# Eight more weight loads in 8 KB reads, two modes per product, and a reordered tail in a windowed-attention and spectral-mix kernel

## The chip, the cores and the metric

One Trainium2 chip, one of its eight cores. The time is device microseconds of one execution, and the median over several executions is given. Lower is better. The profile is of one execution. TensorE is called PE, VectorE DVE, ScalarE ACT, GpSimd POOL and SyncE SP; PEld is PE's loading of the stationary operand. DMAs issued by POOL run in queue q0, those of SP and ACT in q1.

## The reference

```python
# q, k, v: 8 batches x 8 heads x 576 positions x 64, fp32
scores = q @ k.T / 8, kept where 0 <= row - column < 64, else -1e9
x = softmax(scores) @ v              # heads side by side: 8 x 576 x 512
X = rfft(x, axis=1)[:, 0:64]         # 64 modes, complex
Yr = Xr @ w_r - Xi @ w_i             # a 512 x 512 matrix of its own for each mode
Yi = Xr @ w_i + Xi @ w_r
y = irfft(Y, n=576)                  # other modes zero
u = x + y
out = u + relu(u @ w_ch)             # w_ch 512 x 512, fp32
```

The 64 modes have two fp32 matrices each, 128 MiB in all; q, k and v are 27 MiB, the output is 9 MiB.

## The kernel before

Weights are read once. POOL's DMAs cast them from fp32 to bf16 on the way, so 1 MB written means 2 MB read. The modes come in 16 groups of four. Groups 0 to 9 are worked in two halves of the input channels, `hb` 0 (channels 0 to 255) and `hb` 1 (256 to 511); groups 10 to 15 as pairs of whole modes. `wlist` holds the loads in order: first halves of groups 0 to 9 (w_r, w_i each), second halves of groups 0 to 9, then the pairs, the last four pairs of groups (`LAST`, `LAST + 1`) at the end. `load_weights(n)` issues them in this order as far as buffers (`ringA`, `ringB`, lent regions) are free; `due(it)` sets how many are wanted in each step of the attention.

The stage under `manual_schedule` runs attention in 40 units (loop over `it`): transposes of q, k and v (L298), scores (L337, L345), row maxima on DVE (L349), maxima subtracted by a product (L357), exp on ACT (L359), transposes of the weights (L365, L368), product with v (L385, L391, L397), and the forward transform of a batch's half (`do_dft`, L408 and L410, copied by ACT in L413 and L414 to `XQ`). From unit 22 on, `early_step` also does the first half of one group: `mode_half` (L223), 8 products a part (w_r, w_i), each of one mode and 128 channels with 32 columns, on four column groups of PE; the sum goes to `Yacc` (L542). Program order fixes the order on each engine; the engines wait for each other by semaphores, and POOL issues in its program's order.

Then come the second halves. Those of groups 0 and 1 are like the first. Those of groups 2 to 9 (`WIDE = 2`) are loaded by L195: one DMA of 512 KB for two modes, in which a partition reads four rows of a matrix, 8 KB; even partitions hold the one mode and odd ones the other. For that, `wide_modes` spreads the modes' spectra to every second partition, with zeros between (`sprE`, L722 to L741), in `XE`; `mode_wide` (L231) then does one product per mode, in which the other mode's partitions meet zeros: 16 products a part. Loads of L203 (halves of groups 0 and 1, and all first halves) read two rows, 4 KB, per partition and mode; loads of the pairs (L184) read 8 KB.

During the second stage the other work is put between: x times w_ch (L678, L653, L685, L942), inverse tables, and for each group the rows of the spectrum turned (`finish_group`, L755). With the pairs, `mode_pair` (L254) and `finish_pair` do the same; `jobs` holds the products with w_ch of the spectrum's rows (L836, L825, L826), the early sums of x and y (L900, L907) and so on.

The tail begins with the last pair's part: `finish_pair` copies its sum (L770), `turn` transposes it (L785), `put_first` (L790) and `take` (L796) place it; it is multiplied with w_ch (L1205), and `cast_halves` (L702, L703) copies that to `ZL`, the late rows of Z. YL (L1201) holds the late rows of Y. Then tiles of 128 output rows are finished in pairs: `tail_xw` (L976) puts x w_ch in a PSUM bank, `late_u` (L986) and `late_z` (L993) add the late rows for u and for u w_ch, `take_u` (L1007, DVE) and `take_z` (L1011 ACT, L1012 POOL, L1014 DVE) finish them, and SP sends them (L1003). Later tiles go through `full_u` and `full_z` with all rows at once (L1029 to L1063), and `last` does the last pair.

At the very start, eight products of zeros, 128 x 512 each (L432), keep PE busy while the first loads come.

Of the kernel before, what the change touches and what calls it, by code (L numbers as in the profile page):

```python
# [9 lines left out]
FP32 = mybir.dt.float32  # L10
FP32R = mybir.dt.float32r
BF16 = mybir.dt.bfloat16
# [4 lines left out]

NRA = 3
NRB = 5
WARM = 8  # L20
NEG = -1.0e30
MAGIC = 12582912.0
PSAFE = 3.14159
# [3 lines left out]
def kernel(  # L27
# [10 lines left out]
    nc = tc.nc  # L38
# [64 lines left out]
    XA = XA[:, 0:(3 * NW + 2) * B * NMF].rearrange("p (s b m) -> p s b m", b=B, m=NMF)  # L103
    steps += [(grp, hb) for grp in (*range(EARLY, LAST), *range(LAST + 2, NGRP), LAST, LAST + 1) for hb in range(2)]
    WIDE = 2
    NE = 2 * (EARLY - WIDE)
    SHARES = 25, 11, 80, 12
    assert sum(SHARES) == 128
    XE = XE[:, 0:2 * (3 * NW + 2) * B * NE].rearrange("p (h s b m) -> p h s b m", h=2, b=B, m=NE)
    ONES = 3, 0  # L110
    wlist = []
    for at, (grp, hb) in enumerate(steps):
# [37 lines left out]
    def load_weights(n):  # L150
        nonlocal nload
        while nload < len(wlist):
            at, parts, hb, ri = wlist[nload]
            if 2 * n <= sum(len(ps) for ps in parts):
                return
            if nload in lent:
                w = lent[nload]
            else:
                open_to = "a" if at >= 2 * EARLY else "aby" if at < EARLY + 2 else "ab"
                h = min(open_to, key=lambda h: held[h][0] if len(held[h]) == room[h] else -1)  # L160
                if len(held[h]) == room[h]:
                    if held[h][0] not in spent:
                        return
                    held[h].pop(0)
                held[h].append(nload)
                if h == "y":
                    w = lentY
                else:
                    w = {"a": ringA, "b": ringB}[h].tile([128, 4, NJ, DM], BF16, name="wi" if ri else "wr", tag="wt")
            src = moe_w_i if ri else moe_w_r  # L170
            if at >= 2 * EARLY:
                w = w.rearrange("p (m h) j e -> p m (h j) e", m=2)
                p = parts[0][0]
# [13 lines left out]
                wtiles.update(((p + m, ri), w[:, m]) for m in range(2))  # L187
                nload += 1
                n -= 2
                continue  # L190
            if at >= EARLY + WIDE:
                w = w.rearrange("p (q h) j e -> p q (h j e)", q=2)
                for i in range(2):
                    p = parts[0][2 * i]
                    nc.gpsimd.dma_start(  # L195
                        out=w[:, i], in_=src[p:p + 2, HALF:DM, :].rearrange("h (p j) e -> p h (j e)", j=NW))
                    wtiles[p, hb, ri] = w[:, i].rearrange("p (j e) -> p j e", j=NW)
                nload += 1
                n -= 4
                continue  # L200
            to = 0
            for ps in parts:
                nc.gpsimd.dma_start(  # L203
                    out=w[:, to:to + len(ps)],
                    in_=src[ps[0]:ps[-1] + 1, HALF * hb:HALF * hb + HALF, :].rearrange("g (p j) e -> p g j e", j=NJ))
# [25 lines left out]
    def mode_wide(psm, at, ri):  # L231
        grp, hb = steps[at]
        for j in range(NW):
            for g in range(4):
                nc.tensor.matmul(out=psm[32 * g:32 * g + 32, :],  # L235
                                 lhsT=XE[:, g % 2].rearrange("k s b m -> k (s b) m")[:, (3 * j + 1 - ri) * B:(3 * j + 5 - ri) * B,
                                                                                    2 * (grp - WIDE) + g // 2],
                                 rhs=wtiles[4 * grp + g - g % 2, hb, ri][:, j], start=(ri == 0 and j == 0),
                                 stop=(ri == 1 and j == NW - 1), tile_position=(0, 32 * g))
        for i in range(2):  # L240
            wtiles.pop((4 * grp + 2 * i, hb, ri))
        spend(at, ri)

    def mode_pair(psm, at, ri):
        grp, h = steps[at]
# [16 lines left out]
    with tc.manual_schedule():  # L262
# [2 lines left out]
        trigF = maskp.tile([128, NTF, 2 * NM], BF16, name="trigF")  # L265
        mask_t = maskp.tile([128, 3, 4, 128], BF16, name="mask_t")
        rawp = pool("rawp", bufs=2)
        qtp = pool("qtp", bufs=3)
        vtp = pool("vtp")
        vdp = pool("vdp")  # L270
# [158 lines left out]
        nc.vector.memset(idle, 0.0)  # L429
        warm = ps_m.tile([128, DM], FP32, name="warm", tag="misc")  # L430
        for _ in range(WARM):
            nc.tensor.matmul(out=warm, lhsT=idle[:, 0:128], rhs=idle, start=True, stop=True)  # L432

        casts = list(load_by_sp(0, "k", Vflat[1])) + list(load_by_sp(0, "q", Vflat[2]))
        nc.gpsimd.iota(Kf, pattern=[[1, 64]], base=0, channel_multiplier=0,
# [166 lines left out]
        sprE = XL.rearrange("p s b m -> p (s b m)")[:, 0:512].rearrange("p (r h k) -> p r h k", r=2, h=2)  # L602
# [97 lines left out]

        def cast_halves(out, in_):
            nc.vector.tensor_copy(out=out[:, 0:HALF], in_=in_[0][:, 0:HALF])  # L702
            nc.scalar.copy(out=out[:, HALF:DM], in_=in_[1][:, 0:HALF])  # L703

        def whole_modes():
            pts = [[bank("zt"[r == 0]) for j in range(NJ)] for r in range(2)]
# [12 lines left out]
                    nc.vector.tensor_scalar(out=XA[:, i], in0=px[:, 1], scalar1=-1.0, scalar2=None, op0=ALU.mult)  # L719

        def wide_modes():
            nc.vector.memset(sprE, 0.0)  # L722
            for r in range(2):
                for h in range(2):
                    nc.vector.tensor_copy(out=sprE[:, r, h, h::2], in_=ident_bf[:, r::2])
            pts = [[bank("zt"[r == 0]) for j in range(NJ)] for r in range(2)]
            for r in range(2):
                for j in range(NJ):
                    for h in range(2):
                        nc.tensor.matmul(  # L730
                            out=pts[r][j][:, 2 * B * NE * h:2 * B * NE * (h + 1)], lhsT=sprE[:, r, h],
                            rhs=XQ[1][:, 3 * j + 1:3 * j + 3, :, 4 * WIDE:4 * EARLY].rearrange(
                                "p t b (m h) -> p (t b) m h", h=2)[:, :, :, h],
                            start=(h == 0), stop=True, skip_group_check=True)
            nc.vector.memset(XE[:, :, 3 * NW:], 0.0)
            for r in range(2):
                for j in range(NJ):
                    i = 3 * (NJ * r + j)
                    px = pts[r][j].rearrange("p (h t b m) -> p h t b m", h=2, t=2, b=B)
                    nc.scalar.copy(out=XE[:, :, i + 1:i + 3], in_=px)  # L740
                    nc.vector.tensor_scalar(out=XE[:, :, i], in0=px[:, :, 1], scalar1=-1.0, scalar2=None, op0=ALU.mult)  # L741
            lo = 4 * (LAST - EARLY)
            nc.vector.tensor_copy(out=XL, in_=XA[:, :, :, lo:lo + 8])

# [21 lines left out]
        def finish_pair(grp, h, psm):  # L766
            if h == 0:
                late["stg"] = stgpool.tile([128, DM], BF16, name="stg")
            stg = late["stg"][:, HALF * h:HALF * h + HALF]
            nc.vector.tensor_copy(out=stg, in_=psm[:, 0:HALF])  # L770
# [490 lines left out]
```

## Time and profile before

| | |
|---|---|
| median of 3 runs | 430.76 us (430.76 to 431.33) |
| the profiled execution | 430.37 us, its span 428.6 us |
| PE busy | 341.0 us, 80% |
| DVE, ACT, POOL busy | 247.1, 184.6, 113.2 us |
| q0 (POOL's DMAs) | 31424 packets, 81.80 MB written |
| read from HBM | 163.58 MB, 404 GB/s over the span |
| attention ends | about 191 us |
| last weights land | 393.7 us |

GB/s in slices and windows is what the DMA engines write; a casting load reads twice that. The busy share of DMA is a mean over 16 engines and can pass 1, since an engine has several packets under way. In the windows the columns are the stretch, its length, busy time (and instructions) of PE, PEld, DVE, ACT and POOL, the clock granted to PE, the DMA share and GB/s. In the waits a line gives who waited for whom, the sum in us, how often, and the longest. In the timeline a line gives start, duration, engine, line, operation, what is written and read, and in brackets the engine's idle time before and who ended it.

### The profile page before, as it was taken

Reading aid. Unit: us, or ns where it says so; the run is one execution under the profiler, and the core shown is the slowest. Engines: PE = TensorE matmul, PEld = TensorE weight load, DVE = VectorE, ACT = ScalarE, POOL = GpSimd, SP = SyncE. Lnnn points to the kernel's source line nnn. Section 1 sums busy time; section 2 is a strip of 40 time slices with the busy share of each in tenths; the row PEclk is TensorE's granted clock in tenths of the full one; section 3 lists DMA queues with packets and bytes.
Section 4 is the critical chain, followed back from the end, with each engine's and each line's share of the span. In section 5 each row is a group of like instructions: output and inputs, shape, how many; then the busy total and the mean of one; then the engine's idle time right before and its main releaser. Section 6 shows DMA issues by size and latency. Waiting matters only on the chain.

```text
span 428.6 us, 11742 instructions
## 1 busy us (share of the span) xinstructions
PE 341.0 (80%) x5098; PEld 224.9 (52%) x5142; DVE 247.1 (58%) x527; ACT 184.6 (43%) x334; POOL 113.2 (26%) x174
## 2 busy tenths in 40 slices
PE   6889989898999998987628577669675668878994
PEld 3656767676767676663204233346454445445552
DVE  8688777877677675784503212033322333886995
ACT  5655757575676566532401101025222214233663
POOL 8313223222122132112222222121111111120994
PEclk9999999999999999985657767689999986999998
DMA  8999999999999999999999999999999999996698
GB/s 206 211 211 212 211 212 210 212 211 212 211 211 212 213 213 210 213 213 214 213 255 220 213 213 214 207 211 214 214 215 214 214 214 214 213 210 119 241 364 299
DMA packets 37188, 93.30 MB, mean 218 GB/s; under 512 B 2992, under 2 KB 3248, under 8 KB 37136
## 3 DMA queue, kind: packets, MB, share of 16 engines
q0 software_dynamic: 31424, 81.80, 97.9%
q1 hardware_dynamic: 5568, 10.62, 6.8%
q8 instruction: 40, 0.66, 0.6%
q10 hardware_dynamic: 144, 0.13, 0.1%
q14 instruction: 12, 0.10, 0.1%
HBM read 163.58 MB, written 9.44 MB: 404 GB/s over the span
## 4 chain that ended last, share of the span: by engine, by line
DMA 43%; PE 39%; DVE 8%; issue 6%; ACT 3%; POOL 0%; DVEq 0%; SPq 0%; POOLq 0%; ACTq 0%
DMA wr<-in_moe_w_r_dram 23%; DMA wi<-in_moe_w_i_dram 16%; PE tr L298 6%; PE s L345 5%; DMA rawk<-in_k_dram 4%; PE s L357 4%; PE pt L365 4%; PE vb L310 3%; PE o L385 3%; PE s L337 2%; PE psm L223 2%; PE psz L685 2%; PE psm L254 2%; DVE xw L888 1%; PE px L408 1%
## 5 line engine op out<-in xcount | busy, mean ns | idle before, releaser
L685 PE MATMUL psz<-wch,tr 128*128 128x512 f32 x176 | 58.6, 462 | 10.8 <-DMA wch<-in_moe_w_ch_dram 10.0
L349 DVE TENSOR_REDUCE mx<-s 128x4 fp32r<-128x512 f32 x72 | 49.6, 688 | 25.5 <-PE s L345 25.2
L942 DVE CAST xw<-psz 128x512 fp32r<-128x512 f32 x36 | 24.9, 692 | 67.7 <-PE psz L685 67.7
L653 ACT CAST tr<-ptx 128x512 fp32r<-128x512 bf16 x36 | 21.2, 590 | 78.4 <-PE ptx L678 78.4
L359 ACT ACTIVATE p<-s 128x512 bf16<-128x512 f32 x72 | 39.7, 603 | 13.0 <-PE s L357 13.0
L685 PEld LDWEIGHTS psz<-wch,tr 128*128 128x128 f32 x176 | 34.4, 216 | 17.4 <-issue 10.2
L345 PE MATMUL s<-kT,qT 64*64 64x128 bf16 (+1 forms) x576 | 29.2, 221 | 6.7 <-issue 6.7
L302 ACT COPY kT<-tr 128x576 bf16<-128x576 bf16 x32 | 23.2, 724 | 21.4 <-PE tr L298 21.4
L368 DVE COPY pts<-pt 128x1024 bf16<-128x1024 bf16 (+1 forms) x40 | 25.2, 630 | 5.8 <-PE pt L365 4.3
L302 ACT COPY qT<-tr 128x576 bf16<-128x576 bf16 x32 | 23.3, 727 | 11.5 <-PE tr L298 11.5
L235 PEld LDWEIGHTS <-XQ 128*32 128x32 bf16 x256 | 11.4, 147 | 31.9 <-issue 25.5
L345 PEld LDWEIGHTS <-qT 64*64 64x64 bf16 x576 | 18.0, 107 | 17.7 <-issue 17.2
L357 PE MATMUL s<-mx,ident_r 128*128 128x512 f32 x72 | 26.2, 437 | 0.0
L302 ACT COPY vT<-tr 128x576 bf16<-128x576 bf16 x32 | 23.3, 728 | 4.7 <-PE tr L298 4.5
L285 POOL DMA_DIRECT2D rawk<-in_k_dram x15 | 8.1, 538 | 64.3 <-PE tr L298 56.3
L365 PE MATMUL pt<-ident_bf,p 128*128 128x128 bf16 x288 | 23.3, 220 | 1.8 <-issue 1.6
L747 DVE TENSOR_TENSOR stg<-psm,Yfour 128x512 bf16<-128x512 f32 x10 | 6.9, 689 | 30.6 <-PE psm L235 27.1
L254 PEld LDWEIGHTS <-XQ 128*32 128x32 bf16 x256 | 9.4, 149 | 28.4 <-issue 28.1
L235 PE MATMUL psm<-wi,XQ 128*32 128x512 bf16 x128 | 14.9, 507 | 10.5 <-DMA wi<-in_moe_w_i_dram 10.5
L184 POOL DMA_DIRECT2D wi<-in_moe_w_i_dram x14 | 9.5, 683 | 50.2 <-PE psm L254 29.1
L397 DVE TENSOR_TENSOR x_sb<-o,r 128x512 bf16<-128x512 f32 x32 | 22.1, 691 | 1.1
L235 PE MATMUL psm<-wr,XQ 128*32 128x512 bf16 x128 | 15.1, 540 | 7.4 <-DMA wr<-in_moe_w_r_dram 5.4
(277 smaller groups left out, 710.0 us busy)
## 6 DMA issues: line engine op xcount, KB each, us to landing
wi<-in_moe_w_i_dram POOLq DMA_DIRECT2D x21, 1024.0 KB, 14.3
wr<-in_moe_w_r_dram POOLq DMA_DIRECT2D x18, 1024.0 KB, 13.7
wi<-in_moe_w_i_dram POOLq DMA_DIRECT2D x17, 512.0 KB, 19.4
wr<-in_moe_w_r_dram POOLq DMA_DIRECT2D x16, 512.0 KB, 19.4
out_dram<-ut SPq DMA_DIRECT2D x29, 256.0 KB, 3.4
rawv<-in_v_dram POOLq DMA_DIRECT2D x16, 288.0 KB, 15.9
rawk<-in_k_dram POOLq DMA_DIRECT2D x15, 288.0 KB, 14.6
rawq<-in_q_dram POOLq DMA_DIRECT2D x15, 288.0 KB, 14.6
```

The lines of the kernel that those rows point to most:

```text
L235: nc.tensor.matmul(out=psm[32 * g:32 * g + 32, :], lhsT=XE[:, g % 2].rearrange("k s b m -> k (s b) m")[:, (3 * j + 1 - ri) * B:(3 * j + 5 ...
L298: nc.tensor.transpose(out=pt[ro, j, :], in_=raw[ro, TH * half + j, :], identity=ident_bf[ro, ro])
L302: nc.scalar.copy(out=to, in_=pt.rearrange("p j n -> p n j"))
L345: nc.tensor.matmul(out=s[ro, t, lo:128], lhsT=lq, rhs=kT[ro, 64 * n - 64 + lo:64 * n + 64], start=False, stop=True, skip_group_check=True)
L349: nc.vector.tensor_reduce(out=mx, in_=s, axis=AX.X, op=ALU.max, negate=True)
L357: nc.tensor.matmul(out=s, lhsT=ident_r, rhs=mx.unsqueeze(2).to_broadcast([128, 4, 128]), start=False, stop=True, skip_group_check=True)
L359: nc.scalar.activation(out=p[:, 4 * c2:4 * c2 + 4, :], in_=s, func=ACT_F.Exp, scale=EX_SCALE)
L365: nc.tensor.transpose(out=pt[:, t, :], in_=st[u]["p"][:, t, :], identity=ident_bf)
L368: nc.vector.tensor_copy(out=ps[:, 0:nt, :], in_=pt[:, 0:nt, :])
L397: nc.vector.tensor_tensor(out=xo.rearrange("p c (h d) -> p c h d", d=64), in0=ov[:, :, :, 0:64], in1=rb, op=ALU.mult)
L685: nc.tensor.matmul(out=pz, lhsT=tr[:, c, :], rhs=wch[:, c, :], start=(c == 0), stop=(c == NDCH - 1))
L942: nc.vector.tensor_copy(out=XW[i], in_=multiply(tr))
```

## The change

- First halves of groups 6 to 9 (`FIRST_WIDE = 6`) are loaded as the second halves of 2 to 9 are: two DMAs of 512 KB in place of one of 1 MB, 8 KB read per partition and mode. `early_step` uses `mode_wide` for them.
- Before step 6's product, in the step of group 5, `spread_modes` spreads the first halves' spectra to a new tile `XE[0]` and uses both buffers of `ps_m`. The same function replaces the body of `wide_modes`.
- In `XE` seven slots per 128 channels replace three: the even partitions' mode, a slot of zeros, and the odd partitions' mode. One product with 64 columns does both modes, on two column groups of PE: 8 products a part instead of 16.
- 46 zero products of 64 columns instead of 8 of 512.
- Tail: the last pair's sum is copied half by DVE and half by ACT, to a region of its own; `turn` goes 0, 2, 1, 3; in `cast_halves` ACT copies 128 columns and DVE 384; `late_z(0)` stands ahead of `late_u(1)`.

```diff
-WARM = 8
+WARM = 46
+    FIRST_WIDE = 6
+    wide_from = (FIRST_WIDE, WIDE)
+    XE = {1: XE[:, 0:(7 * NW + 2) * B * NE].rearrange("p (s b m) -> p s b m", b=B, m=NE)}
...
-            if at >= EARLY + WIDE:
+            if steps[at][0] >= wide_from[hb]:
                 w = w.rearrange("p (q h) j e -> p q (h j e)", q=2)
                 for i in range(2):
                     p = parts[0][2 * i]
                     nc.gpsimd.dma_start(
+                        out=w[:, i],
+                        in_=src[p:p + 2, HALF * hb:HALF * hb + HALF, :].rearrange("h (p j) e -> p h (j e)", j=NW))
...
         for j in range(NW):
+            for i in range(2):
+                nc.tensor.matmul(out=psm[64 * i:64 * i + 64, :],
+                                 lhsT=XE[hb].rearrange("k s b m -> k (s b) m")[:, (7 * j + 1 - ri) * B:(7 * j + 9 - ri) * B,
+                                                                               2 * (grp - wide_from[hb]) + i],
+                                 rhs=wtiles[4 * grp + 2 * i, hb, ri][:, j], start=(ri == 0 and j == 0),
+                                 stop=(ri == 1 and j == NW - 1), tile_position=(0, 64 * i))
...
+    def spread_modes(hb, spread, pts):
+        xe, m0 = XE[hb], wide_from[hb]
+        n = 2 * (EARLY - m0)
+        nc.vector.memset(spread, 0.0)
+        for r in range(2):
+            nc.vector.tensor_copy(out=spread[:, 128 * r + 1:128 * r + 128:2], in_=ident_bf[:, r::2])
+        for r in range(2):
+            for j in range(NJ):
+                px = pts[r][j].rearrange("p (h x) -> p h x", h=2)
+                for h in range(2):
+                    nc.tensor.matmul(
+                        out=px[:, h], lhsT=spread[:, 128 * r + 1 - h:128 * r + 129 - h],
+                        rhs=XQ[hb][:, 3 * j + 1:3 * j + 3, :, 4 * m0:4 * EARLY].rearrange(
+                            "p t b (m h) -> p (t b) m h", h=2)[:, :, :, h],
+                        start=(h == 0), stop=True, skip_group_check=True)
+        nc.vector.memset(xe[:, 0:7 * NW].rearrange("p (j s) b m -> p j s b m", s=7)[:, :, 3], 0.0)
+        nc.vector.memset(xe[:, 7 * NW:], 0.0)
+        for r in range(2):
+            for j in range(NJ):
+                i = 7 * (NJ * r + j)
+                px = pts[r][j].rearrange("p (h t b m) -> p h t b m", h=2, t=2, b=B)
+                at = [xe[:, i + t:i + t + 8].rearrange("p (h s) b m -> p h s b m", h=2) for t in range(2)]
+                nc.scalar.copy(out=at[1][:, :, 0:2], in_=px)
+                nc.vector.tensor_scalar(out=at[0][:, :, 0], in0=px[:, :, 1], scalar1=-1.0, scalar2=None, op0=ALU.mult)
...
-            nc.tensor.matmul(out=warm, lhsT=idle[:, 0:128], rhs=idle, start=True, stop=True)
+            nc.tensor.matmul(out=warm[:, 0:64], lhsT=idle[:, 0:128], rhs=idle[:, 0:64], start=True, stop=True)
...
+            if grp == FIRST_WIDE - 1:
+                both = [ps_m.tile([128, DM], FP32, name="spread", tag="misc") for r in range(2)]
+                spread_modes(0, spread, [[t[:, HALF * j:HALF * j + HALF] for j in range(NJ)] for t in both])
...
-                mode_half(psm, grp, ri)
+                (mode_half if grp < FIRST_WIDE else mode_wide)(psm, grp, ri)
...
-            nc.scalar.copy(out=out[:, HALF:DM], in_=in_[1][:, 0:HALF])
+            nc.scalar.copy(out=out[:, HALF + 128:DM], in_=in_[1][:, 128:HALF])
+            nc.vector.tensor_copy(out=out[:, HALF:HALF + 128], in_=in_[1][:, 0:128])
...
+            if end and i == 3:
+                stg = XL.rearrange("p s b m -> p (s b m)")[:, 0:HALF]
+                nc.vector.tensor_copy(out=stg[:, 0:128], in_=psm[:, 0:128])
+                nc.scalar.copy(out=stg[:, 128:HALF], in_=psm[:, 128:HALF])
+            else:
+                nc.vector.tensor_copy(out=stg, in_=psm[:, 0:HALF])
...
-                for c in range(NDCH):
+                for c in (0, 2, 1, 3):
...
         banks_u(1)
+        late_z(0)
         late_u(1)
-        late_z(0)
```

More of the change, by code (lines that the diff above doesn't have):

```diff
@@ L108 @@
     assert sum(SHARES) == 128
-    XE = XE[:, 0:2 * (3 * NW + 2) * B * NE].rearrange("p (h s b m) -> p h s b m", h=2, b=B, m=NE)
+    XE = {1: XE[:, 0:(7 * NW + 2) * B * NE].rearrange("p (s b m) -> p s b m", b=B, m=NE)}
     ONES = 3, 0
@@ L195, in load_weights @@
                     nc.gpsimd.dma_start(
-                        out=w[:, i], in_=src[p:p + 2, HALF:DM, :].rearrange("h (p j) e -> p h (j e)", j=NW))
+                        out=w[:, i],
+                        in_=src[p:p + 2, HALF * hb:HALF * hb + HALF, :].rearrange("h (p j) e -> p h (j e)", j=NW))
                     wtiles[p, hb, ri] = w[:, i].rearrange("p (j e) -> p j e", j=NW)
@@ L233, in mode_wide @@
         for j in range(NW):
[L234 to L239, printed above, removed]
+            for i in range(2):
[4 more added lines that the diff above has]
+                                 stop=(ri == 1 and j == NW - 1), tile_position=(0, 64 * i))
         for i in range(2):
@@ L267 @@
         rawp = pool("rawp", bufs=2)
+        NF = 2 * (EARLY - FIRST_WIDE)
+        XE[0] = maskp.tile([128, 7 * NW + 2, B, NF], BF16, name="XF")
+        spread = maskp.tile([128, 257], BF16, name="spread")
         qtp = pool("qtp", bufs=3)
@@ L601 @@
         XL = zpool.tile([128, 3 * NW + 2, B, 8], BF16, name="XL")
-        sprE = XL.rearrange("p s b m -> p (s b m)")[:, 0:512].rearrange("p (r h k) -> p r h k", r=2, h=2)
+        sprE = XL.rearrange("p s b m -> p (s b m)")[:, 0:257]
         trpool = pool("trpool", bufs=2, reuse_waits="tile")
@@ L721, in wide_modes @@
         def wide_modes():
[L722 to L741, printed above, removed]
+            spread_modes(1, sprE, [[bank("zt"[r == 0]) for j in range(NJ)] for r in range(2)])
             lo = 4 * (LAST - EARLY)
@@ L769, in finish_pair @@
             stg = late["stg"][:, HALF * h:HALF * h + HALF]
-            nc.vector.tensor_copy(out=stg, in_=psm[:, 0:HALF])
             i = 2 * (grp % 2) + h
             end = grp - grp % 2 == LAST
+            if end and i == 3:
[4 more added lines that the diff above has]
+                nc.vector.tensor_copy(out=stg, in_=psm[:, 0:HALF])
             if i == (1 if end else 0):
```

## The prediction

> **What bounds the kernel now.** I read the page first (slices, queues, chain), then the windows of the load stages, who waited for whom on POOL, and the timeline of the last 35 us.
>
> ```profile
> DMA  8999999999999999999999999999999999996698
> q0 software_dynamic: 31424, 81.80, 97.9%
> DMA 43%; PE 39%; DVE 8%; issue 6%; ACT 3%; POOL 0%; DVEq 0%; SPq 0%; POOLq 0%; ACTq 0%
> ```
>
> The DMA slices are full from the second to the 36th, that is to about 390 us, while the clock and PE row of the page go up and down beneath them. The chain names PE for 39%, but a chain follows one path: where PE and the loads run side by side it may take either. Whether a late PE costs time depends on whether the load queue ever runs empty. The windows of a stage with loads of half matrices (second row) and with the loads of 8 KB reads (third row), and POOL's waits from 105 to 260 us:
>
> ```profile
> 171.40:186.50 15.10, 14.63 (x277) 10.45 (x281) 12.09 (x27) 8.30 (x17) 2.35 (x4) 1.00 1.13 213
> 228.40:272.80 44.40, 31.69 (x246) 15.60 (x244) 9.82 (x19) 5.08 (x9) 10.36 (x18) 0.73 1.06 213
> ```
> ```profile
> POOL wi L195 <- DMA wi<-in_moe_w_i_dram: 18.9, 9, 4.1
> POOL wi L203 <- PE psm L223: 9.7, 2, 8.2
> ```
>
> In both stages the queue moves about 213 GB/s, with PE at a clock of 1.00 or 0.73: the loads don't follow PE. POOL itself waits up to 8.2 us for a buffer, and nothing happens, because what it issues stands in line anyway. I sorted the trace's packet records of q0 by start and counted them off load by load. The time between the end of an issue and its first packet is then the work still ahead of it: 9.7 us or more for issues at 128 to 203 us (12.7 or more after 157), 7.1 us at the least before 230 us (at 63 us), 3.3 at 274 us, 2.6 at 374 us, never zero until the last load. So the time is: one unbroken load stream to 393.3 us, and a tail behind it.
>
> ```profile
> 383.48 10.26 DMA wi<-in_moe_w_i_dram
> 393.74 0.04 issue
> 393.78 0.44 PE psm L254 x4
> ```
>
> This is the chain's joint: the last quarter MB lands at 393.7 us and the tail begins. It lasts 34.8 us.
>
> **The change part by part.**
>
> *Loads.* The first halves of groups 6 to 9 are eight loads of 1 MB (written), each 512 packets of 2 KB; they become sixteen of 512 KB with 128 packets of 4 KB. From the same count, first packet to the next load's first packet, those eight take 5.07, 5.12, 5.17, 5.16, 5.03, 5.11, 5.18 and 5.11 us: 40.95. The form they become stands in the trace: 18 loads of L195 from 228.45 to 272.84 us take 2.466 us each, so 16 take 39.46. Gain at most 1.49. At least: three half loads in a row with no q, k, v between (171.45 to 186.48 us) take 5.01 each, 0.08 over two wide ones; times 8 is 0.64. Part of the eight's length is handing over to a q, k or v load and the instruction fetches, which are denser under attention, and stays. I take 1.1, between the ends, nearer to the eight's own rows. The eight extra DMAs are in it: 2 x 2.466 against 4.90 for a 1 MB load of L184 is 0.03 us each. On POOL two issues of 0.58 replace one of 0.75: +0.41 x 8 = 3.3 us, on an engine that waits.
>
> The Trainium skill speaks against this split: "DMA: Bandwidth & Descriptors", section "Rules for kernel authors", asks for 1 MiB and more per DMA, and its fit has about 2 us fixed in each. By that the eight extra ones would cost up to 16 us; the trace's 0.03 disagrees, as the queue is never empty. The same page, "Why small descriptors are slow", gives some 3 cycles per packet beside a beat per 32 bytes: 131 against 259 beats, an estimate of 1.2% of 41 us, 0.5 us of gain, less than the rows' range.
>
> *PE under attention.* A half step of L223 runs 1.05 us for both parts in the chain, two rounds of 512 columns each. The new form has four rounds in two column groups: about +0.9 to +1.05 us a step, four steps, some 4 us. The spreading before step 6 happens once: it takes both buffers of ps_m; eight products (a row of the same kind, L730, has four in 1.0 us at 0.6 clock), then four ACT copies (0.37 each, L413's size) and four DVE ones (0.28) before PE has its bank: 2 to 3 us stall. Attention ends some 6 to 7 us later, at 197 instead of 191. What is queued behind it: POOL's issues that wait for L223 and L298. They had 9.7 us in hand at 156 us, when about 4 of the 7 have come together, and 12.7 or more later; they keep 5. Cost zero; without that cover 7 us. Between 205 and 270 us PE needs about 4.2 us of each 9.8 us group for the modes, beside L685, and catches up before the margin shrinks to 3.3.
>
> *Modes of second halves.* 16 products a part become 8, in two column groups instead of four: the same four rounds (L1038, two groups, four products in 0.62 us, shows them side by side). No time, less issue. The rewritten spreading there has two copies fewer on DVE and wider memsets: within 0.3 us, under the same cover.
>
> *Short zero products.* 8 x 427 ns end at 4.8 us now. 46 short ones: at least 46 x 38 ns (64-wide transposes, 18 in 0.69) = 1.7; at most load 142 ns plus 53 = 9.0 us. PE's first real work waits for a cast until 5.4. The worst is 4.8 us late, and the first issue behind it (9.08 us) has 6.9 us of queue ahead. Zero at both ends.
>
> *Tail.* The rows that matter:
>
> ```profile
> 394.26 0.42 DVE L770 CAST stg<-psm 128x256 bf16<-128x256 f32 x1 [1.28 <-PE psm L254]
> ...
> 396.04 0.42 DVE L702 CAST tr<-psz 128x256 fp32r<-128x256 f32 x1
> ...
> 396.51 0.37 ACT L703 CAST tr<-psz 128x256 fp32r<-128x256 f32 x1 [1.31 <-PE psz L1205]
> ...
> 396.63 0.37 PE L986 MATMUL psy<-stg,trigL 32*128 32x512 bf16 x1
> ...
> 396.93 0.50 PE L993 MATMUL pst<-tr,trigLr 32*128 32x512 f32 x2
> 397.36 0.73 PE L976 MATMUL psz<-xw,ident_r 128*128 128x512 f32 x2
> ...
> 398.14 1.28 POOL L1012 TENSOR_TENSOR utx<-x_sb,utx 128x512 f32<-128x512 f32 x1 [0.46 <-DVE x_sb L1007]
> ...
> 398.55 1.08 ACT L1011 ACTIVATE ut<-psz 128x512 f32<-128x512 f32 x2 [0.50 <-PE psz L993]
> ...
> 399.64 2.52 POOL L1012 TENSOR_TENSOR ut<-XQ,ut 128x512 f32<-128x512 f32 x2 [0.22 <-ACT ut L1011]
> ```
>
> From 399.64 to 417.3 POOL adds without a gap, so the tail's pace hangs on its first two starts. The split stg copy: 128 columns cost DVE 0.29 (0.42 for 256, 0.69 for 512) and ACT 0.26: 0.13 earlier, of which about 0.1 is left because L976 ahead of the turns still runs. The copy of ZL: ready 0.1 earlier, but POOL's first add waits for DVE's L1007, which waits for L986: nothing. late_z(0) ahead of late_u(1): L986's pair (0.23 from 396.40 to 396.63) filled PE's wait for ZL; now it stands before L976 and the second tile's L993, which ACT (398.55) and POOL's second add (399.64) wait for: +0.15, less the 0.1 of ZL. Sum of the tail: -0.1 + 0.05 = -0.05, between -0.25 and +0.3.
>
> *Sum.* 1.1 + 0.05 = 1.15 us less. The profiled execution took 430.37 (span 428.6 and 1.8 around it), 0.4 under the median 430.76. Against its own time 429.2; against the median, which I predict, **429.6**.
>
> **Rivals.**
>
> *The pitch falls only by the lower end, or the end gives it back* (chance 0.26). The windows above show 213 in both stages, which speaks for a small gain: 0.64 gives 430.1. Or the compute that runs beside the last loads takes over: PE waits for the last load only 0.5 us at 393.78, and the chain from 354.45 to 382.40 is PE, DVE and ACT. Against it: that chain starts at a landing, at 354.40, which comes earlier too. If it stretches by 0.5, 430.1 as well. The page's 3 cycles per packet, by the way, would give 430.3, within no change.
>
> *Attention is late enough to drain the queue* (0.10, slower). Place: POOL's issues between 150 and 205 us behind L223. Price: one us for each us beyond 12.7; with the gain of 1.15 and 0.86 to be seen it decides at about 14.7 us of delay. I count 7. For it: PE is busy 14.6 of 15.1 us there, so nothing is caught up before 191. At 15.2 us, 2.5 - 1.15 over the median: 432.1.
>
> *Splitting exposes each DMA's latency* (0.02). A DMA that finds the queue empty lands 2.2 us after issue (Yall<-stg, 32 KB): eight times, 448. Only with an empty queue. It is the 1 MiB rule's case; the trace so far is against it.
>
> **Numbers.** Likeliest 0.62: 429.6, own range 429.0 to 429.9. About 0.2% (0.86 us) can be told from no change: faster is under 429.9, slower over 431.6. Faster 0.62, same 0.26, slower 0.12. The range for 8 in 10 goes from 428.7 (1.49 and 0.25 and some noise of runs, which spread 0.6) to 430.9, which takes in the first rival and leaves out most of the second.
>
> **What would show it.** q0 with some 1,900 packets fewer; the last load landing near 392.6; psm steps 6 to 9 at about 2 us; attention ending near 197 with the DMA slices still full; the tail still 34.6 to 35.1 us. I am wrong if a DMA slice before 380 us shows a hole, if the last landing hasn't moved, or if the tail differs by over 0.5.

## The result: 0.3% slower, and where it shows

The changed kernel takes 431.94 us (median of 10 runs, 431.79 to 432.37), the kernel before beside it 430.77 (10 runs, 430.04 to 431.33). The ratio is 1.0031, 95% interval 1.0023 to 1.0039. The prediction was 429.6 us and its range ended at 430.9, so the time lies above both: the change made the kernel slower by 1.2 us, where I expected 1.15 us less.

The profiled execution of after took 432.23 us, its span is 430.4 (before: 430.37 and 428.6). The page of after, the rows that answer to those of before (slices, load queue, shares of the chain):

```profile
DMA  8999999999999999999999999999999999994896
q0 software_dynamic: 29504, 81.80, 96.8%
DMA 42%; PE 37%; DVE 7%; issue 6%; ACT 4%; POOL 1%; DVEq 0%; POOLq 0%
```

The load queue has 1,920 packets fewer, as forecast, and the DMA slices are still full from the second to the 36th: no hole. Two stages of the load stream in after, by windows (columns: window, its length, then busy time and instructions of PE, weight loads, DVE, ACT and POOL, the granted clock, the DMA share, GB/s):

```profile
171.40:186.50 15.10, 14.46 (x255) 10.82 (x257) 10.21 (x24) 8.21 (x14) 4.31 (x7) 1.00 1.12 211
228.40:272.80 44.40, 31.67 (x161) 18.47 (x161) 9.82 (x19) 5.08 (x9) 10.36 (x18) 0.73 1.06 213
```

By the packet records the first window holds 4 KB reads in both kernels (the 8 KB reads of first halves end at 170.6 us in after), and moves 211 GB/s where it moved 213; the second holds 8 KB reads in both. The changed loads run from 113 to 171 us. A window inside that stretch, before and then after:

```profile
126.00:166.00 40.00, 37.59 (x839) 27.90 (x844) 29.04 (x62) 26.82 (x50) 10.42 (x17) 1.00 1.12 212
126.00:166.00 40.00, 35.30 (x693) 25.67 (x699) 26.61 (x64) 23.28 (x45) 11.40 (x20) 0.91 1.08 213
```

So the 8 KB reads moved 213 GB/s there and the 4 KB reads 212: a gain, and a small one. The joint of load stream and tail, from the chain of waits:

```profile
383.26 10.31 DMA wi<-in_moe_w_i_dram
393.57 0.04 issue
393.61 0.44 PE psm L282 x4
```

The last load lands at 393.57 us, 0.17 earlier than before. From there to the end of the span it is 36.8 us, where it was 34.8. So 2 us were lost behind the loads. The timeline of that stretch in after (start, length, engine, line, and in brackets the idle time before the instruction and what ended it):

```profile
394.09 0.29 DVE L790 CAST XL<-psm 128x128 bf16<-128x128 f32 x1 [1.34 <-PE psm L282]
...
394.41 0.27 ACT L791 CAST XL<-psm 128x128 bf16<-128x128 f32 x1 [1.92 <-DVE XL L790]
...
396.00 0.42 DVE L736 CAST tr<-psz 128x256 fp32r<-128x256 f32 x1
...
396.47 0.27 ACT L737 CAST tr<-psz 128x128 fp32r<-128x128 f32 x1 [1.30 <-PE psz L1226]
...
396.77 0.29 DVE L738 CAST tr<-psz 128x128 fp32r<-128x128 f32 x1 [0.34 <-ACT tr L737]
...
397.12 0.50 PE L1014 MATMUL pst<-tr,trigLr 32*128 32x512 f32 x2 [0.36 <-DVE tr L738]
...
398.38 1.29 POOL L1033 TENSOR_TENSOR utx<-x_sb,utx 128x512 f32<-128x512 f32 x1 [0.76 <-ACT utx L1032]
```

The two halves of each split copy run one after the other: L791 starts when L790 has ended, L738 when L737 has. `late_z(0)` (L1014) begins 3.55 us behind the landing, where it was 3.19. That is 0.36 us of delay, and 0.17 of it is made up by the earlier landing. The rest is at the very end. The instructions that close the program are all put down to the line that opens the tile context. Here that line in after (POOLq is GpSimd's sequencer, SPq SyncE's; then operation, count, duration in ns as min/median/max, first and last start):

```profile
L1277 POOLq EVENT_SEMAPHORE  x4: 17/17/17, 429.7 to 430.3; - x4
L1277 POOLq DRAIN  x3: 46/102/7538, 422.1 to 430.2; - x3
L1277 SPq DRAIN  x3: 7/7/7, 427.7 to 429.9; - x3
```

and in before:

```profile
L1256 POOLq EVENT_SEMAPHORE  x4: 17/17/17, 427.8 to 428.5; - x4
L1256 POOLq DRAIN  x3: 46/102/2552, 421.8 to 428.3; - x3
L1256 SPq DRAIN  x3: 7/7/7, 427.8 to 428.1; - x3
```

SyncE, which waits for the outputs, begins its first two drains by 427.8 us in both kernels (the second at 427.80 in after and 427.82 in before, in the trace's own records). GpSimd's closing drain opens 0.04 us ahead of its last sum (at 422.1 in after, 421.8 in before), so that sum's 1.28 us are part of its length. It lasts 7.54 us and not 2.55. It ends at 429.65, 1.9 us behind SyncE, and only then does GpSimd's closing wait begin (429.7, before 427.8). In before the drain ended at 424.36, 3.5 us ahead of SyncE, and set nothing. No view of the prediction had looked at it.

### The profile page after: what moved, and what is told of

Same layout as the page of the kernel before. It is cut to its first block, busy times and chain, and to the rows that moved or that the text cites. A ratio compares the mean times of both kernels' runs of the same rounds, so it can differ in the third digit from the quotient of the medians.

```text
span 430.4 us, 11604 instructions
## 1 busy us (share of the span) xinstructions
PE 345.6 (80%) x5016; PEld 236.2 (55%) x5060; DVE 248.5 (58%) x536; ACT 186.2 (43%) x339; POOL 116.7 (27%) x182
## 3 DMA queue, kind: packets, MB, share of 16 engines
q0 software_dynamic: 29504, 81.80, 96.8%
## 4 chain that ended last, share of the span: by engine, by line
DMA 42%; PE 37%; DVE 7%; issue 6%; ACT 4%; POOL 1%; DVEq 0%; POOLq 0%
DMA wr<-in_moe_w_r_dram 22%; DMA wi<-in_moe_w_i_dram 12%; DMA rawk<-in_k_dram 7%; PE tr L329 5%; PE s L376 4%; PE s L388 3%; PE pt L396 3%; PE vb L341 3%; PE o L416 2%; PE psm L226 2%; PE psz L719 2%; PE psm L238 2%; PE s L368 2%; PE psm L282 2%; DVE xw L909 1%
## 5 line engine op out<-in xcount | busy, mean ns | idle before, releaser
L719 PE MATMUL psz<-wch,tr 128*128 128x512 f32 x176 | 61.6, 481 | 9.6 <-DMA wch<-in_moe_w_ch_dram 8.8
L719 PEld LDWEIGHTS psz<-wch,tr 128*128 128x128 f32 x176 | 36.1, 226 | 16.3 <-issue 8.9
L238 PEld LDWEIGHTS <-XQ 128*64 128x64 bf16 x128 | 14.4, 204 | 24.7 <-issue 18.6
L282 PEld LDWEIGHTS <-XQ 128*32 128x32 bf16 x256 | 9.6, 151 | 26.7 <-issue 26.5
L197 POOL DMA_DIRECT2D wi<-in_moe_w_i_dram x22 | 12.8, 585 | 41.6 <-DMA wi<-in_moe_w_i_dram 16.7
L186 POOL DMA_DIRECT2D wi<-in_moe_w_i_dram x14 | 9.5, 684 | 51.7 <-PE psm L282 31.8
L197 POOL DMA_DIRECT2D wr<-in_moe_w_r_dram x24 | 14.2, 602 | 31.7 <-DMA wr<-in_moe_w_r_dram 22.7
L238 PE MATMUL psm<-wr,XQ 128*64 128x512 bf16 x64 | 15.0, 549 | 7.1 <-DMA wr<-in_moe_w_r_dram 5.6
```

What stands on the lines that cost most here:

```text
L197: nc.gpsimd.dma_start(out=w[:, i], in_=src[p:p + 2, HALF * hb:HALF * hb + HALF, :].rearrange("h (p j) e -> p h (j e)", j=NW))
L238: nc.tensor.matmul(out=psm[64 * i:64 * i + 64, :], lhsT=XE[hb].rearrange("k s b m -> k (s b) m")[:, (7 * j + 1 - ri) * B:(7 * j + 9 - ri) * B,
L719: nc.tensor.matmul(out=pz, lhsT=tr[:, c, :], rhs=wch[:, c, :], start=(c == 0), stop=(c == NDCH - 1))
```

## The experiments

The same figures were taken of every kernel: the landing of the last weight load (from the chain), the last output's issue, the length of GpSimd's closing drain, and the time against the kernel before.

**Which part of the change moves the end.** `loads_only` is the changed kernel without the tail edits and the short zero products; `tail_only` is the kernel before with the tail edits; `pool8` and `after_pool32` add instructions on GpSimd.

```diff
 loads_only, against after
-            nc.scalar.copy(out=out[:, HALF + 128:DM], in_=in_[1][:, 128:HALF])
-            nc.vector.tensor_copy(out=out[:, HALF:HALF + 128], in_=in_[1][:, 0:128])
+            nc.scalar.copy(out=out[:, HALF:DM], in_=in_[1][:, 0:HALF])
...
-WARM = 46
+WARM = 8
 tail_only, against before
-            nc.scalar.copy(out=out[:, HALF:DM], in_=in_[1][:, 0:HALF])
+            nc.scalar.copy(out=out[:, HALF + 128:DM], in_=in_[1][:, 128:HALF])
+            nc.vector.tensor_copy(out=out[:, HALF:HALF + 128], in_=in_[1][:, 0:128])
...
+        late_z(0)
         late_u(1)
-        late_z(0)
 pool8, against before; after_pool32 has range(32), against after
                 if half == 0:
+                    for _ in range(8):
+                        nc.gpsimd.memset(junk, 0.0)
                     nc.gpsimd.dma_start(out=wch, ...)
```

> The changed kernel with its tail edits and its short zero products undone: the kernel before with the first halves of groups 6 to 9 in 8 KB reads, two modes in one product, and the spreading under the attention. It tells which part moved the end. Three theories of GpSimd's last drain (2.55 us before, 7.54 us after, and the end of the program 1.85 us later behind it). T1, the length of GpSimd's program: the 8 further instructions push its last ones into a block of code that is fetched only at the very end. T2, the number of loads that GpSimd issued: the drain has more of their bookkeeping to end. T3, the edits of the tail. T1 and T2: the drain is about 7.5 us here too, the time 1.0 to 1.5 us over the kernel before (431.8 to 432.3). T3: the drain is about 2.5 us and the time 0 to 0.3 under the kernel before (430.5 to 430.8). In each of them the last load lands 0.1 to 0.3 us earlier than before (393.45 to 393.65), and late_z(0) begins as far behind it as before, 3.2 us.

> The kernel before with the tail edits alone (the split copies, the order of the four transposes, late_z(0) ahead of late_u(1)); loads and products as before. If the two halves of a split copy run one after the other, as in the trace of after, late_z(0) begins 0.3 to 0.4 us later behind the last load's landing than before (3.55 against 3.19 us), and the last output is issued 0.3 to 0.5 us later. T1 and T2 (GpSimd's instructions and loads are those of before): its last drain stays near 2.5 us, and the time is 0.0 to 0.5 over the kernel before (430.8 to 431.3). T3: the drain is about 7.5 us and the time 1.2 to 1.9 over it.

> The kernel before with 8 one-column memsets on GpSimd, put ahead of the load of moe_w_ch behind the attention, where the loads are issued 10 us ahead of their transfer. They write a tile that nothing reads. No load is added, and nothing else is changed. T1 (the length of GpSimd's program): the last drain grows from 2.5 to about 7.5 us and the time by 1.2 to 1.9 us (432.0 to 432.6). T2 (the number of loads) and T3 (the tail): the drain stays near 2.5 us, the time within 0.2 of the kernel before.

> The changed kernel with 32 one-column memsets on GpSimd, at the same place as in pool8. T1: the border of the last block of code now falls some 24 instructions ahead of where it fell in the kernel before, among the last sums and not behind them; it is fetched while GpSimd still has work, the last drain is back near 2.5 us, and the time falls by 1.0 to 1.9 us to 430.0 to 430.9 although instructions are added. T2: the drain stays at 7.5 us or more and the time at 431.9. T3: as T2.

Measured: `loads_only` 432.08 us, ratio 1.0028 (1.0017 to 1.0039), landing 393.31, `late_z(0)` 3.19 behind it as in before. `tail_only` 430.91, ratio 0.9998 (0.9986 to 1.0010), `late_z(0)` 3.56 behind the landing. `pool8` 430.73, ratio 0.9998 (0.9988 to 1.0007). `after_pool32` 432.30, ratio 1.0036 (1.0024 to 1.0048). The drains, in the same view as above, one line of each kernel in this order:

```profile
L1271 POOLq DRAIN  x3: 46/102/7537, 421.5 to 429.6; - x3
```
```profile
L1262 POOLq DRAIN  x3: 46/102/2553, 422.3 to 428.8; - x3
```
```profile
L1259 POOLq DRAIN  x3: 46/102/2562, 422.3 to 429.0; - x3
```
```profile
L1280 POOLq DRAIN  x3: 46/102/7545, 421.8 to 429.9; - x3
```

The drain goes with the loads alone. T1 falls twice: 8 instructions more do nothing, and 32 more mend nothing. T3 falls with `tail_only`. The length is 7.54 or 2.55 us to about a hundredth, wherever the kernel's end lies. That speaks for work of a fixed length that starts with the drain, and against a wait for something that happens at the end. The tail edits show their 0.36 us behind the landing, but `tail_only`'s time doesn't tell it from nothing.

**Transfers or packets.** The changed loads are 8 transfers more and 1,920 packets fewer (120 for each of the 16 DMA engines).

```diff
 split8, against before (loads_split16, against loads_only: hb == 0 and grp in (1, 2, 4, 5))
-                parts = [[(p, p + 1, p + 2, p + 3)]]
+                parts = [[(p, p + 1), (p + 2, p + 3)]] if (hb == 0 and grp >= 6) else [[(p, p + 1, p + 2, p + 3)]]
 first_wide8, against loads_only (and the PSUM slices of the spreading cut to their new width)
-    FIRST_WIDE = 6
+    FIRST_WIDE = 8
 second_wide4, against loads_only (likewise)
-    WIDE = 2
+    WIDE = 4
```

> GpSimd's last drain was 7.54 us in each kernel with the changed loads (146 transfers issued by GpSimd, 29,504 packets on their queue, 1,844 per transfer engine) and 2.55 us in each with the old ones (138 transfers, 31,424 packets, 1,964 per engine), whatever the number of other instructions. Two theories are left: T2a, the number of transfers sets it; T2b, the number of packets sets it, fewer packets giving the longer drain. This kernel is the one before, with each of the 8 first-half loads of groups 6 to 9 issued as two transfers of two modes, packets as before: 146 transfers, 31,552 packets (1,972 per engine: one closing packet per engine and transfer more). T2a: the drain is 7.5 us and the time 1 to 1.9 us over the kernel before. T2b: the drain is at most 2.55 us and the time within 0.3 of the kernel before; what lies between them is then the price of 8 more transfers.

> loads_only with the 8 KB reads of first halves from group 8 on and not from group 6: 4 further transfers and not 8 (142), 30,464 packets (1,904 per engine). T2a, if the drain grows by 0.62 us with each transfer (4.99 us over 8): 5.0 us, and the time about 0.3 to 0.8 under loads_only; if it is a step, 2.55 or 7.54. T2b, linear between the two ends (1,964: 2.55 and 1,844: 7.54): 5.0 us as well. So this run tells a step from a slope, and second_wide4 tells transfers from packets.

> loads_only with the second halves of groups 2 and 3 back in 4 KB reads and single transfers: 142 transfers, 4 fewer than loads_only, and 30,464 packets by the same count as first_wide8, but from other groups and later in the stream. T2a and T2b both put its drain where first_wide8 has it. A drain that differs from first_wide8 by more than 0.2 us would speak against both and for the place of the loads in the stream.

> loads_only with 8 other first-half loads (groups 1, 2, 4 and 5) issued as two transfers each, their packets as before: 154 transfers, 29,632 packets (1,852 per engine). T2a as a slope: the drain is 12.5 us and the time 5 us over loads_only; as a step: 7.5. T2b: 7.2 us (0.042 us for each packet of an engine), and the time that of loads_only within 0.4.

Measured: `split8` 430.73 us, ratio 0.9998 (0.9989 to 1.0007); `first_wide8` 431.83, 1.0021 (1.0010 to 1.0031); `second_wide4` 431.87, 1.0030 (1.0008 to 1.0051); `loads_split16` 431.87, 1.0021 (1.0011 to 1.0031). The drains in that order:

```profile
L1256 POOLq DRAIN  x3: 46/102/2313, 422.2 to 428.6; - x3
```
```profile
L1271 POOLq DRAIN  x3: 46/102/7697, 421.7 to 429.9; - x3
```
```profile
L1271 POOLq DRAIN  x3: 46/102/7203, 422.2 to 429.9; - x3
```
```profile
L1271 POOLq DRAIN  x3: 46/102/7618, 421.4 to 429.5; - x3
```

The plain number of transfers falls with `split8`: 146 of them, and the drain is shorter than before's. A straight line over packets falls as well: 1,904 packets per engine give 7.70 and 7.20, not 5.0, and the two differ by 0.49, which by its expectation speaks for the place of the loads in the stream. What I made of the short ones was T5: that the two short drains (84 and 76 packets short of 2,048) are 30.4 ns for each missing packet. That was a line through two points.

**Adding a transfer without touching the loads.** It moves single words behind the last weight load, on the load queue; I call it the filler.

```diff
 loads_fill128, against loads_only; before_fill128 the same against before; before_fill64 and loads_fill64 with 0:16:2
+    junk = consts.tile([128, 32], FP32, name="junk")
...
+                if nload == len(wlist) - 1:
+                    nc.gpsimd.dma_start(out=junk[:, ::2], in_=moe_w_ch[0:128, 0:32:2])
```

> loads_only with one transfer more, issued by GpSimd right behind the last weight load: 2,048 single words (128 partitions by 16) into a tile that nothing reads, 128 packets and a closing one for each transfer engine, so 1,973 packets per engine in all. T2b in a closer form, T5: the two short drains were 2.55 us at 1,964 packets and 2.31 us at 1,972, that is 30.4 ns for each packet that is missing to 2,048 (84 x 30.4 = 2.55, 76 x 30.4 = 2.31), and with 144 to 204 missing it ends only 2.4 to 2.8 us behind the last output. T5: the drain is 2.3 us (75 x 30.4 ns), it ends ahead of the outputs, and the time is 0.3 to 0.8 us under the kernel before (430.1 to 430.6), with the last load landing where loads_only has it (393.0). If the drain depends on which loads were made and not on the count (T6), it stays near 7.5 us and the time at 431.9 or above. The words may also hold back the first transfer of the tail, which would show as a later last sum (more than 28.6 us behind the last load's landing).

> The kernel before with such a transfer of 1,024 words: 64 packets and a closing one per engine, 2,029 in all, 19 short of 2,048. T5: the drain is no longer set by the missing packets (19 x 30.4 ns = 0.6 us) and is that of the last sum alone, 1.3 us; the time is that of the kernel before within 0.3, as the drain ended ahead of the outputs there too. T6: the drain stays at 2.55 us.

> The kernel before with the transfer of 2,048 words: 2,093 packets per engine, 45 past 2,048. T5: the count has turned over and hundreds are missing to the next border, so the drain is the long one, ending 2.4 us or more behind the last output, and the time is 1 us or more over the kernel before (431.8 or more), with the loads, the products and the tail of before. T6: the drain stays at 2.55 us and the time at that of before, plus at most 0.5 for the transfer.

Measured: `loads_fill128` 430.12 us, ratio 0.9975 (0.9954 to 0.9995); `before_fill64` 431.06, 1.0007 (0.9995 to 1.0019); `before_fill128` 430.48, 0.9997 (0.9985 to 1.0010). The drains:

```profile
L1274 POOLq DRAIN  x3: 46/102/2230, 421.7 to 427.9; - x3
L1274 SPq DRAIN  x3: 7/7/7, 427.3 to 427.6; - x3
```
```profile
L1259 POOLq DRAIN  x3: 46/102/2645, 422.2 to 429.2; - x3
```
```profile
L1259 POOLq DRAIN  x3: 46/102/2642, 422.1 to 429.7; - x3
```

One further transfer takes 5.3 us off the drain of `loads_only`. The drain now ends at 423.9, ahead of SyncE's first at 427.3, and the kernel is a little faster than the one before. By medians that is 430.12 against 430.78; two of the 29 runs of before, at 433.72 and 434.55, make the ratio of 0.9975 look larger.

The filler is not the 128 packets per engine of my expectations. The page of `loads_fill128` counts 48 packets more on the load queue than the 29,504 of `loads_only`:

```profile
q0 software_dynamic: 29552, 81.81, 97.2%
```

In the trace's records these are 16 closing packets and 32 of 256 bytes, 64 words each. The 128 are single words for each engine, and it is words that the counts below go by.

T6 (it depends on which loads were made) falls. But T5 falls too: the fillers on the kernel before should have given 1.3 us and a long drain, and both gave 2.64. The list of drains gave the next idea. They lie on steps of about 0.08 us: 7.20, 7.54, 7.62, 7.70 (4, 1 and 1 steps), 2.23, 2.31, 2.55, 2.64 (1, 3 and 1). `before_fill64` and `before_fill128` differ in words and not in transfers, and are alike. The idea is that something of 0.08 us is done once for a transfer, for those transfers since some turning point. The size of the last transfer alone is not what shortens the drain: `before_fill128` has the same 2,048 words as `loads_fill128`, and its drain is one step longer than before's.

**The turning point.** T7 was put to two tests beside the whole changed kernel with the filler.

```diff
 before_tiny8, against before
+                if nload == len(wlist) - 1:
+                    for i in range(8):
+                        nc.gpsimd.dma_start(out=junk[0:16, i:i + 1], in_=moe_w_ch[0:16, i:i + 1])
 after_fill128, against after: the two lines of loads_fill128
```

> T5 (a price for each packet missing to 2,048) fell with before_fill64 and before_fill128. What is left, T7: GpSimd's last drain pays about 0.082 us for each transfer that it has issued since its record of them was last cleared, and the record is cleared when about 1,008 packets per transfer engine have been issued since. Worked out for the ten drains: a count of the transfers left over since the clearing gives 8 for the kernel before (second clearing at 366 us) and 74 for loads_only (one clearing, at 165 us), a difference of 66, measured (7.54 - 2.55) / 0.082 = 61. This kernel is the one before with 8 transfers of 16 words each behind the last weight load (2 packets per engine each, far too few for another clearing). T7: 8 transfers more are left over, the drain is 2.55 + 8 x 0.082 = 3.2 us, the time within 0.3 of the kernel before. If the drain goes by packets and not by transfers, it changes by no more than 0.1 (2.45 to 2.65 us).

> loads_only with 1,024 words behind the last weight load, half of what loads_fill128 had: 65 packets per engine. T7: by the same count the record has some 100 packets of room left at that point, so 65 do not clear it and the drain is that of loads_only with one transfer more, 7.62 us, the time about 431.9 (1 us over the kernel before). If what shortened the drain in loads_fill128 was the mere presence of a late transfer, or something proportional to its size, the drain is near 2.3 us, or near 4.9 us.

> The whole changed kernel (split copies, new order, short zero products included) with the 2,048 words of loads_fill128 behind its last weight load. T7: the drain is 2.2 to 2.3 us, and with it gone from the end the tail decides again: the last output is issued 31.1 us or more behind the last load's landing (30.7 in loads_fill128), and the time is 0.2 to 0.5 us over loads_fill128 and 0 to 0.5 under the kernel before (430.3 to 430.8). If the tail edits cost nothing at the end, the time is that of loads_fill128 within 0.1.

Measured: `before_tiny8` 430.28 us, ratio 1.0010 (0.9987 to 1.0033); `loads_fill64` 431.56, 1.0025 (1.0015 to 1.0034); `after_fill128` 430.19, 0.9997 (0.9986 to 1.0007). The drains:

```profile
L1260 POOLq DRAIN  x3: 46/102/3205, 421.6 to 428.1; - x3
```
```profile
L1274 POOLq DRAIN  x3: 46/102/7612, 421.0 to 429.1; - x3
```
```profile
L1280 POOLq DRAIN  x3: 46/102/2235, 421.6 to 427.8; - x3
```

Eight tiny transfers behind the turning point cost 0.65 us (3.205 for 3.2 forecast); eight more that were issued early in the program, in `loads_split16`, had cost 0.08 (7.618 against 7.537). Half a filler doesn't turn it and counts as one transfer more (7.612 for 7.62); a whole one turns it, in the changed kernel too (2.235).

A count goes along each kernel's transfers. Each is taken as its packets per engine (a filler as its words) and two for closing, and everything that had landed is struck off when the next would pass 1,078. It leaves 8 transfers in before, 73 or 74 in `loads_only` and after, 18 in `before_tiny8`, 7 in the two changed kernels with the full filler. A line over these numbers, 1.83 us and 0.077 for each, meets all sixteen drains within 0.14 us. With the packets of the profile in place of words it does not work: `loads_fill128`, whose drain is short, would be at some 990 for each engine, and `second_wide4`, whose drain is long, is at 1,048.

So it is shown that a late transfer costs some 0.08 us in the drain, and that 2,048 words turn the long drain where 1,024 do not. That it is a record which GpSimd keeps of its transfers is my reading, since no row shows the clearing itself. The border and the two closing ones are fitted to the same sixteen drains (990 with one closing does nearly as well), and the counts shift by a few with what is taken as landed.

By this count before strikes off a second time at about 370 us, some eight transfers from its last, and goes into the end with few transfers left. The 120 packets per engine that the 8 KB reads save keep after from coming so far: all its transfers since 164 us still count when the program closes.

In `after_fill128` the drain no longer decides, and the change is worth nothing that can be told: 0.9997. Its last output is issued 30.94 us behind the landing, in `loads_fill128` 30.59. `loads_fill128`, the changed loads with the filler and without the tail edits, has the lowest median of the three.

## Why the prediction was wrong, step by step

- *One unbroken load stream bounds the kernel:* right. No slice before 380 us shows a hole, and the loads stayed ahead. The sign of being wrong that the prediction named for the tail did come: 36.8 us where it allowed 34.6 to 35.1.
- *PE under attention costs nothing:* right in size and cover. A half step of the modes takes 2.00 us in after (1.12 before), attention's last product starts at 196.8 us (191.0 before; forecast 197), and the queue stays full: by the packet records the load with the least work ahead of it between 128 and 230 us, issued at 157, still had 7.1 us of it (the prediction kept 5). The rival of a drained queue did not occur; I had it at 0.10.
- *Loads, 1.1 us less (0.64 to 1.49):* too large, the low end too. The pair of profiles shows 0.17 at the landing. Over all profiles, the seven with before's loads land at 393.50 to 394.31 (mean 393.97), the seven with the eight changed ones at 392.80 to 393.57 (mean 393.27): 0.70 less, give or take 0.32 from the spread within each seven. But the stretch with the changed loads gives less than half of that. Counted off the packet records of the same fourteen, from the load that starts at 103.6 us in before to the one at 228.45, it takes 124.85 to 125.01 us with before's loads and 124.52 to 124.65 with the changed ones: 0.30 less, give or take 0.06. Where the other 0.4 comes from is not shown. The step that failed is the measuring of a load from its own first packet to the next load's. The changed loads did get short by that measure (4.0 to 4.6 us for a MB), but the q, k and v loads behind them took some 1.7 us and not 1.4: the time between two loads is shared by the two. Why the low end, 0.08 us for each load from loads in a row, came out as half of that stays open. The estimate from the Trainium skill ("DMA: Bandwidth & Descriptors", "Why small descriptors are slow"), 0.5 us, lies inside what the landings show and above what the stretch shows.
- *Eight transfers more at 0.03 us each:* in the stream this holds. `split8` adds them alone and lands at 394.13, where the other six with before's loads land at 393.50 to 394.31. The Trainium skill's rule of 1 MiB and more per DMA (same page, "Rules for kernel authors") would put up to 16 us there, by the prediction's estimate from some 2 us fixed in each; `split8`'s 430.73 us against 430.94 disagrees with the price. The rule itself is hardly broken here, as a load of 512 KB written still reads 1 MB. What I did not ask is what a transfer costs after it has landed: some 0.08 us in the closing drain, if it lies behind the turning point.
- *Modes of second halves and short zero products, nothing:* no run takes them alone. In after the zero products end at 3.8 us, and PE then waits for a cast until 6.6, so they hold nothing up.
- *Tail, -0.05 us (-0.25 to +0.3):* +0.36, wrong in sign. The step that failed is "0.13 earlier" for the split copy and "ready 0.1 earlier" for ZL's, both of which take the two halves to run side by side. In before the halves of `cast_halves` read two PSUM tiles and each waits for PE alone; in after both pieces of the second read one tile, and the program itself makes the second engine wait for the first (by a semaphore, ACT's for L738 and DVE's for L791). ZL is complete 3.49 us behind the landing and not 3.14. The Trainium skill has this in "PSUM — Partial Sum Buffer", section "PSUM bank collisions raise a hardware error": the compiler's scheduler puts a dependency between instructions of two engines on one bank and the same partitions, reads by ScalarE and VectorE too. The trace agrees: L738 starts 0.03 us after L737's end. The trace of before had shown it as well, in four casts that all write `trz`: the first two read one tile and take turns, the other two read two tiles and run side by side, so it is the reading that counts.

```profile
392.50 0.21 ACT L796 CAST trz<-psp 128x64 fp32r<-128x64 f32 x1 [2.12 <-PE psp L785]
392.75 0.23 DVE L796 CAST trz<-psp 128x64 fp32r<-128x64 f32 x1 [0.36 <-ACT trz L796]
...
394.99 0.21 ACT L796 CAST trz<-psp 128x64 fp32r<-128x64 f32 x1 [2.27 <-PE psm L785]
395.04 0.22 DVE L796 CAST trz<-psm 128x64 fp32r<-128x64 f32 x1 [0.36 <-PE psm L785]
```

- *The end of the program:* the step that failed most, since the prediction has none for it and so puts it at nothing. I took the 34.8 us from the landing to the end as one tail that ends with the outputs. It ended with the later of two things, the outputs (427.8) and GpSimd's drain (424.4), and the second had 3.5 us of room. The change used 5.0, as the drain grew from 2.55 to 7.54. This is the term that made the kernel slower: 1.9 us.
- *Sum:* -0.70 for the landing, +0.36 for the tail, +1.9 for the drain make +1.6; the medians differ by 1.2, and single profiles spread by 0.3 on each term. With the drain out of the way (`after_fill128`) the first two nearly cancel, and so does the time. The first rival, that the end gives the gain back, was right in kind, but by another mechanism and at a price that I had not reached.

## What to carry to other kernels

Read how a program closes before you call the last output its end: an engine's closing drain has a length and some room, and a change far away can use the room up. A saving in one count (packets) may keep another from passing a threshold, so ask what else goes by that count; here one transfer of 2,048 single words was worth 2 us (432.08 against 430.12). And before a copy is split over two engines, look whether both pieces read one PSUM tile: here those went one after the other, and the split cost the second start.

## What was not expected of the hardware

GpSimd's closing drain depends on the transfers that it has issued, long after they have landed: 2.2 to 7.7 us in these kernels. Eight more near the end made it 0.65 us longer, about 0.08 for each, and one transfer of 2,048 words made it 5.3 us shorter, where 1,024 words did not. The words were cheap: GpSimd issued them in 1.18 us, and the last load and the tail behind it (`late_z(0)` 3.19 us after the landing) did not move. Reads of 8 KB in place of 4 KB were worth 0.30 us over 8 MB with the queue never empty, under 1% of those loads' 41 us.
